# Remainder rows of k and v: four heads on each half of the partitions, multiplied in quarters of the array

## The chip, the cores and the metric

The kernel runs on one core of a Trainium2 chip. The metric is the device time of one execution in microseconds (us), as a median over runs; lower is better. The core has TensorE (PE in the profile, with PEld for its weight loads), VectorE (DVE), ScalarE (ACT), GpSimd (POOL) and SyncE (SP), whose queue issues most of the DMA transfers.

## What is computed

A linear attention block without softmax, a root-mean-square norm, and then an MLP mixer over tokens and channels. All inputs are f32 or wider, all results f32.

```python
batch, n_heads, seq, head_dim = (8, 8, 576, 64)      # q, k, v
d_tok, d_ch = (256, 1536)                            # the mixer's weights
kv = np.einsum('bhsd,bhse->bhde', k, v)
out = np.einsum('bhsd,bhde->bhse', q, kv)
rms = np.sqrt(np.mean(out * out, axis=-1, keepdims=True) + 1e-06)
x = (out / rms * g_norm)                             # then (B,H,S,D) -> (B,S,H*D)
h = np.maximum(x.transpose(0, 2, 1) @ w_tok1, 0.0) @ w_tok2
u = x + h.transpose(0, 2, 1)
y = u + np.maximum(u @ w_ch1, 0.0) @ w_ch2
```

The step of interest is `kv`: for each batch and head, k transposed times v, a sum over 576 rows that gives 64 by 64.

## The kernel before

Batches are worked in four pairs; the two of a pair are its sides 0 and 1. A batch's k is held as `k_in[side]`, 128 partitions by 5 row groups by 512 columns (8 heads of 64), and v as `v_in[side]`. `J` = 4 of the groups hold rows 0 to 511, four rows to a partition; the fifth (`JJ` = 5) holds the remainder, the last `HF` = 64 rows. The two buffers of a side are used again by every pair, so the batches of pair n+1 are loaded (`load`, steps `l0`, `l1`) after the products of pair n have read them. `load` issues four things on SP's queue in this order: k's 512 rows (1 MB), k's remainder, v's 512 rows, v's remainder. In the first pair (b < 2) the remainder takes another way: 64 rows of k and v are laid on 128 partitions as half rows and spread out with zeros by `spread_k`. From pair 1 on `load_rem` puts the 64 remainder rows on partitions 0 to 63, all 512 columns, in two transfers of 32 rows by 2 KB. Partitions 64 to 127 of that group are zero: `zero_rows` clears them once on POOL during pair 0 (steps `zz0`, `zz1`).

`kv(side, half)` multiplies for four heads (`half` 0: columns 0 to 255, `half` 1: columns 256 to 511). Each matmul takes 128 rows and 64 columns of k as weights and 64 columns of v as moving operand, and goes to one column half of the array (`h` 0 or 1, output partitions 0 to 63 or 64 to 127), so that two run side by side. Per half there are 2 x 5 x 2 = 20 matmuls, per batch 40, 8 of them for the remainder group, over 128 partitions of which 64 are zero. The two halves accumulate in two PSUM tiles of the pool `kv`. `evict` (steps `e00` to `e11`) copies each to `kvp[side]` on ScalarE, and `attend` multiplies q by it, as 64 x 64 matmuls that go round the four quarters of the array.

The order of all work is written out by hand in lists of step names: `start` (pair 0), `middle` (pair 1 beside the token mixing of pair 0), `steady` (pairs 2 and 3). The steps that are named below: `kvSH` k by v of side S, half H; `eSH` its copy; `aC` the attention of row chunk C (`a4` the remainder rows of q); `qCH`, `gCH`, `tCH` squares on ScalarE, gain and sum on VectorE; `dCT` and `sCT` the scaling of chunk C on VectorE or ScalarE, `pCT` on POOL; `hST` the first product of the token mixing, `hr` its remainder rows and ReLUs, `uN` the second product of tile N with its addition and store; `-` before a name is a step of the pair before; `fN` fetches a block of the channel weights, a number plays that many steps of their decoding on ScalarE and VectorE. Every matmul is issued by one helper, line 136 of the profile; SP's DMAs by line 124, ScalarE's plain copies by line 133. Each engine does its instructions in the order in which they are issued.

Of the kernel before, what the change touches and what calls it, by code (L numbers as in the profile page):

```python
# [20 lines left out]
def kernel(  # L21
# [32 lines left out]
    nc = tc.nc  # L54
    P = 128
    B, S, DM = k.shape
    D = g_norm.shape[0]
# [3 lines left out]
    J, JJ, HF, Q = 4, 5, 64, 32  # L61
    LO = P * J
# [3 lines left out]
    DH = DM // 2  # L66
# [41 lines left out]
    k_in = [inp.tile([P, JJ, DM], F32, name=f"k_in{i}") for i in range(2)]  # L108
    v_in = [inp.tile([P, JJ, DM], F32, name=f"v_in{i}") for i in range(2)]
# [5 lines left out]
    def do(f, *a, **kw):  # L115
        return lambda: f(*a, **kw)
# [4 lines left out]
    keep = tc.keep_in_program_order  # L121

    def dma(o, i, engine=nc.sync):
        keep(engine.dma_start(o, i))
# [10 lines left out]
    def matmul(*a, **kw):  # L135
        keep(nc.tensor.matmul(*a, **kw))  # L136
# [7 lines left out]
    def load_rem(dst, t, b):  # L144
        if b < 2:
            at = ds(DH if dst is k_in[b] else 0, DH)
            dma(v_in[b][:, J, at], t[b, LO:].rearrange("r (a d) -> (r a) d", a=2))
            return
        for n in range(0, HF, Q):
            dma(dst[n:n + Q, J], t[b, LO + n:LO + n + Q].rearrange("(r e) d -> e r d", e=8))  # L150

    def load(b):

        if b >= B:
            return

        pairs = ((k_in[b % 2], k), (v_in[b % 2], v))
        if b > 1:
            for dst, t in pairs:
                load_rows(dst, t, b)  # L160
                load_rem(dst, t, b)
        else:
            for f in (load_rows, load_rem):
                for dst, t in pairs:
                    f(dst, t, b)
# [119 lines left out]
    def t_sums(b):  # L285

        def step(o, x, y):
            return lambda: tensor_add(b(o), b(x), b(y), ALU.subtract)

        return [step(5, 7, 1), step(6, 3, 5), step(7, 3, 7), step(4, 2, 6)]  # L290
# [96 lines left out]
    def attention(pair, groups):  # L387


        bank, stat, kv_ps = {}, {}, {}  # L390
# [4 lines left out]
        whole = pair == 0  # L395

        def kv(side, half, js=range(JJ)):
            kk, vv = k_in[side], v_in[side]
            if js[0]:
                o = kv_ps[side, half]  # L400
            elif whole:
                o = kv_ps[side, half] = zeroed[half]
            else:
                o = kv_ps[side, half] = ps["kv"].tile([P, 2, P], F32, name="ps_kv", tag="kv")
            split = len(js) < JJ
            for i in range(2):
                for j in js:
                    for h in range(2):
                        at = ds(half * DH + i * P + h * D, D)
                        matmul(o[ds(h * D, D), i, ds(h * D if whole else 0, D)], lhsT=kk[:, j, at],  # L410
                               rhs=vv[:, j, ds(i * P + h * D, D) if whole and j == J else at],
                               start=(j == 0 and not (split and i)), stop=(j == JJ - 1), skip_group_check=True)

        def evict(side, half):
            n = P if whole else D
# [156 lines left out]
        steps = {}  # L572
        for s in range(2):
            for h in range(2):
                steps |= {f"ka{s}{h}": do(kv, s, h, range(J)), f"kb{s}{h}": do(kv, s, h, range(J, JJ)),
                          f"kv{s}{h}": do(kv, s, h), f"e{s}{h}": do(evict, s, h),
                          f"l{s}": do(load, 2 * pair + 2 + s)}
            steps |= {f"lq{s}": do(load_q, 2 * pair + 2 + s), f"lr{s}": do(load_q_rest, 2 * pair + 2 + s)}
        for c in range(5):
            if whole:  # L580
# [740 lines left out]
    def play(lines, after={}, **stages):  # L1321

        for name in " ".join(lines).split():
            if name.isdigit():
                for _ in range(int(name)):
                    next(stages["rounding"], lambda: None)()
            elif name[0] == "-":
                stages["before"][name[1:]]()  # L1330
            else:
                next(stages[s][name] for s in ("attention", "mixing", "more")
                     if name in stages.get(s, ()))()
# [32 lines left out]
        else:  # L1366
            keep(nc.scalar.activation(o, i, AF.Copy, scale=own[:, half:half + 1]))

    def zero_rows(side):
        for t in (k_in, v_in):  # L1370
            keep(nc.gpsimd.memset(t[side][HF:, J], 0.0))

    root = stats.tile([P, 1], F32, name="root")
    keep(nc.vector.memset(root, 1.0))
    keep(nc.scalar.activation(root, root, AF.Sqrt))
    def spread_g():
# [3 lines left out]
        copy(g_sb[:, 0], o[:, :D])  # L1380

    start = [
# [6 lines left out]
    middle = [  # L1389
# [5 lines left out]
    steady = [[  # L1395
# [10 lines left out]

    attentions = [attention(0, ((0,), (1,), (2,), (3,), (4,)))]
    attentions += [attention(p, ((0, 1), (2, 4), (3,))) for p in range(1, B // 2)]

    mixings = [token_mixing(p, (2, 4, 6)) for p in range(B // 2 - 1)]  # L1410
    mixings.append(token_mixing(B // 2 - 1, range(2, 9), (0, 1)))
    more = {f"w{n}{k}": f for n, b in enumerate(first_rows[:1] + tok1[1:] + tok2 + first_rows[1:]) for k, f in enumerate(b)}
# [6 lines left out]
    def keep_warm(n):  # L1419
# [3 lines left out]
        for _ in range(n):  # L1423
# [2 lines left out]
    more |= {f"j{n}": do(keep_warm, n) for n in (4, 5, 21)}  # L1426
    more["gs"] = spread_g
    more |= {f"zk{side}{half}": do(spread_k, side, half) for side in range(2) for half in range(2)}
    more |= {f"zz{side}": do(zero_rows, side) for side in range(2)}
    play(start, attention=attentions[0], mixing=mixings[0], more=more)  # L1430
    play(middle, attention=attentions[1], mixing=mixings[0], before=attentions[0],
         more=more, rounding=rounding)
    for n in range(1, B // 2 - 1):
        play(steady[n - 1], attention=attentions[n + 1], mixing=mixings[n], before=attentions[n] | {"u8": mixings[n - 1]["u8"]},
             more=more, rounding=rounding)
# [16 lines left out]
    more = {f"c{i}": f for i, f in enumerate(t_sums(lambda n: uT[0][:, SB[n]]))}  # L1452
# [98 lines left out]
```

## Time and profile before

| | us |
|---|---|
| median of 3 runs (769.81 to 770.58) | 770.58 |
| the profiled execution | 769.76 |
| its span | 767.9 |
| k by v, 640 records in all, ScalarE's 15 copies of it | 20.9 and 266 ns each |

The profile is one execution on the chip, with the start and length of every instruction. The granted TensorE clock is full throughout. The span falls in two parts: up to about 151 us the attention and the first three pairs' mixing over tokens, thereafter the last pair's mixing and the mixing over channels. The change touches the first part alone, from pair 1 (its first k by v starts at 36 us) to pair 3 (its last at 130 us).

How to read it: the page gives each engine's busy time; the chain of waits goes back from the last instruction to what released it; views in order of time list start, length, engine, line, what is written and read, and a count, and in square brackets the idle time before with its releaser. Engine names with a q are the queue, where DMAs are issued. A form such as 128*64 is the part of the array that a matmul uses, rows by columns.

### The profile page before, as it was taken

To read this page: it belongs to the slowest core of one execution; us is meant where nothing else is said; L and a number is where in the kernel's file an instruction comes from. 1 tells how busy PE (TensorE), PEld (TensorE's weight loads), DVE (VectorE), ACT (ScalarE), POOL (GpSimd) and SP (SyncE) were. 2 spreads that over 40 slices of the span, in tenths; PEclk is the share of its full clock that TensorE was granted. 3 is DMA by queue.
4 is the path that set the end of the run, shared out by engine and by line. 5 is a ranking of instruction groups with operands and counts; after the bars stand their busy time and mean duration, and the time that the engine had idled before them with its cause. 6 is when DMAs were issued, how large, how long until landed. Compare 5 with 4: busy or idle time off the path is not lost.

```text
span 767.9 us, 12737 instructions
## 1 busy us (share of the span) xinstructions
PE 761.9 (99%) x4694; PEld 615.4 (80%) x4694; DVE 644.9 (84%) x958; ACT 279.5 (36%) x563; POOL 112.8 (15%) x125
## 2 busy tenths in 40 slices
PE   9999999999999999999999999999999999999997
PEld 8655555446888888888888888888888888888887
DVE  4868886997757779899968989997898997798996
ACT  3656666773210332512234241123352223325221
POOL 1003030204410000002240002042000227000204
PEclk9999999999999999999999999999999999999999
DMA  9999997599699785589997578999659889755679
GB/s 356 379 366 382 353 376 281 178 326 340 244 290 318 291 284 167 172 271 217 221 230 251 154 226 213 261 185 265 195 154 295 159 227 211 199 150 158 156 188 120
DMA packets 137981, 188.28 MB, mean 245 GB/s; under 512 B 48704, under 2 KB 95808, under 8 KB 135872
## 3 DMA queue, kind: packets, MB, share of 16 engines
q1 hardware_dynamic: 102240, 168.72, 68.3%
q0 software_dynamic: 34848, 18.36, 15.9%
q8 instruction: 38, 0.62, 0.3%
q10 hardware_dynamic: 832, 0.39, 0.2%
q14 instruction: 23, 0.19, 0.1%
HBM read 138.28 MB, written 49.15 MB: 244 GB/s over the span
## 4 chain that ended last, share of the span: by engine, by line
PE 96%; DMA 2%; DVE 1%; SPq 0%; ACT 0%; issue 0%; DVEq 0%
PE ps_d L136 28%; PE ps_b L136 19%; PE ps_a L136 19%; PE ps_u L136 8%; PE ps_h L136 8%; PE ps_v L136 5%; PE ps_c L136 3%; PE ps_w L136 2%; PE ps_kv L136 2%; PE ps_o L136 2%; DMA raw<-in_moe_w_tok_dram 1%; DMA v_in<-in_k_dram 1%; PE ps_r L136 0%; DVE x L494 0%; DVE ms L522 0%; DVE w_tok L211 0%
## 5 line engine op out<-in xcount | busy, mean ns | idle before, releaser
L136 PE MATMUL ps_d<-ui,w 128*128 128x256 f32 x504 | 118.6, 379 | 0.0
L136 PEld LDWEIGHTS ps_d<-ui,w 128*128 128x128 f32 x504 | 96.0, 190 | 12.8
L133 ACT COPY ps_d<-ps_a 128x768 f32<-128x768 f32 (+1 forms) x56 | 32.0, 572 | 199.9 <-PE ps_a L136 196.9
L127 DVE TENSOR_TENSOR v<-v,v 128x1536 f32<-128x1536 f32 (+2 forms) x70 | 103.3, 1483 | 0.3
L136 PE MATMUL ps_b<-sv,w 128*128 128x256 f32 x324 | 78.9, 380 | 0.0
L136 PE MATMUL ps_a<-v,w 128*128 128x256 f32 x324 | 78.8, 379 | 0.0
L1275 POOL DMA_DIRECT2D out_dram<-us x24 | 26.8, 1835 | 291.8 <-ACT p L133 286.5
L136 PEld LDWEIGHTS ps_b<-sv,w 128*128 128x128 f32 x324 | 61.3, 190 | 8.8 <-issue 0.6
L136 PEld LDWEIGHTS ps_a<-v,w 128*128 128x128 f32 x324 | 61.7, 190 | 8.2
L136 PE MATMUL ps_u<-h,w_tok 128*128 128x512 f32 (+1 forms) x160 | 64.7, 599 | 0.0
L136 PE MATMUL ps_d<-v,w 128*128 128x256 f32 x258 | 62.7, 379 | 0.0
L130 ACT ACTIVATE v<-v 128x768 f32<-128x768 f32 (+1 forms) x54 | 42.6, 822 | 55.1 <-DVE v L127 52.3
L136 PE MATMUL ps_h<-x,w_tok 128*128 128x512 f32 x128 | 57.6, 601 | 0.7 <-DVE w_tok L211 0.6
L1275 POOL DMA_DIRECT2D out_dram<-r x40 | 41.3, 1926 | 102.0 <-ACT p L133 80.3
L136 PE MATMUL ps_d<-sv,w 128*128 128x256 f32 x228 | 55.4, 379 | 0.0
L136 PEld LDWEIGHTS ps_d<-v,w 128*128 128x128 f32 x258 | 49.1, 190 | 6.5
L136 PEld LDWEIGHTS ps_u<-h,w_tok 128*128 128x128 f32 (+1 forms) x160 | 25.7, 179 | 31.1 <-issue 26.7
L136 PEld LDWEIGHTS ps_d<-sv,w 128*128 128x128 f32 x228 | 43.4, 190 | 5.8
L136 PE MATMUL ps_a<-uT,w 128*128 128x256 f32 x192 | 46.7, 379 | 0.0
L136 PEld LDWEIGHTS ps_h<-x,w_tok 128*128 128x128 f32 x128 | 23.5, 190 | 28.3 <-issue 24.3
L136 PE MATMUL ps_b<-ui,w 128*128 128x256 f32 x168 | 40.9, 379 | 0.0
L136 PEld LDWEIGHTS ps_a<-uT,w 128*128 128x128 f32 x192 | 36.5, 190 | 4.9
(178 smaller groups left out, 1299.1 us busy)
## 6 DMA issues: line engine op xcount, KB each, us to landing
w<-parts SPq DMA_DIRECT2D x168, 384.0 KB
w<-parts SPq DMA_DIRECT2D x56, 192.0 KB
uT<-blocks SPq DMA_DIRECT2D x36, 256.0 KB
k_in<-in_k_dram SPq DMA_DIRECT2D x8, 1024.0 KB
v_in<-in_v_dram SPq DMA_DIRECT2D x8, 1024.0 KB
qT<-in_q_dram SPq DMA_DIRECT2D x8, 1024.0 KB
out_dram<-x POOLq DMA_DIRECT2D x16, 512.0 KB, 7.2
raw<-in_moe_w_ch_dram SPq DMA_DIRECT2D x8, 768.0 KB
```

The lines of the kernel that those rows point to most:

```text
L127: keep(engine.tensor_tensor(out=o, in0=a, in1=b, op=op))
L130: keep(nc.scalar.activation(o, a, AF.Relu))
L133: keep(nc.scalar.copy(o, a))
L136: keep(nc.tensor.matmul(*a, **kw))
L1275: keep(nc.gpsimd.dma_start(to, t()[ds(b * Q, Q), at].rearrange("p n l j -> p n (l j)"), accum_op=ALU.add))
```

## The change

The remainder rows of pairs 1 to 3 are laid out another way: heads 0 to 3 on partitions 0 to 63, heads 4 to 7 on partitions 64 to 127, 256 columns each. So a batch's remainder of k comes in four transfers of 32 rows by 1 KB, and so does v's; nothing is cleared. `kv` leaves out the remainder group in these pairs, and a new step `kr0` or `kr1` (`kv_rem`) multiplies it for both halves: 8 matmuls of 64 rows by 64 columns, in which the halves of the heads stand on the row halves of the array and the two heads of a pair on the column halves. It adds to both accumulators, so both copies `e` follow it. In the lists `kr` stands behind both `kv` steps of its side; at side 0 of pairs 2 and 3 the step `-u8` is moved between `kv01` and `kr0`, ahead of the copies and `-d40`, and `-a3` then follows `kr0` on TensorE.

```diff
@@ load_rem
-        for n in range(0, HF, Q):
-            dma(dst[n:n + Q, J], t[b, LO + n:LO + n + Q].rearrange("(r e) d -> e r d", e=8))
+        for a in range(2):
+            for n in range(0, HF, Q):
+                dma(dst[ds(a * HF + n, Q), J, :DH],
+                    t[b, ds(LO + n, Q), ts(a, DH)].rearrange("(r e) d -> e r d", e=8))
@@ kv
-                               start=(j == 0 and not (split and i)), stop=(j == JJ - 1), skip_group_check=True)
+                               start=(j == 0 and not (i and (split or not whole))),
+                               stop=(j == JJ - 1), skip_group_check=True)
+
+        def kv_rem(side):
+            o = [kv_ps[side, a] for a in range(2)]
+            for i in range(2):
+                for h in range(2):
+                    for a in range(2):
+                        r, at = ds(a * HF, HF), ds(i * P + h * D, D)
+                        matmul(o[a][ds(h * D, D), i, :D], lhsT=k_in[side][r, J, at], rhs=v_in[side][r, J, at],
+                               start=False, stop=True, skip_group_check=True)
@@ the steps
-                          f"kv{s}{h}": do(kv, s, h), f"e{s}{h}": do(evict, s, h),
+                          f"kv{s}{h}": do(kv, s, h, range(JJ if whole else J)), f"e{s}{h}": do(evict, s, h),
...
+            steps[f"kr{s}"] = do(kv_rem, s)
@@ the first pair (zz1 likewise)
-    def zero_rows(side):
-        for t in (k_in, v_in):
-            keep(nc.gpsimd.memset(t[side][HF:, J], 0.0))
...
-        "j21 zk00 zk01 ka00 ka01 gs kb00 e00 kb01 e01 zz0 eg0 eg1 l0 w01 w02 w03 w04 j4",
+        "j21 zk00 zk01 ka00 ka01 gs kb00 e00 kb01 e01 eg0 eg1 l0 w01 w02 w03 w04 j4",
@@ middle
-        "h100 h110 h101 h111 w31 w22 w23 w24", "kv00 e00 -lq1 w32 w33 w34",
-        "h102 h112 h103 h113 w41 w42 w43 w44", "kv01 e01", "hr l0 z2",
+        "h100 h110 h101 h111 w31 w22 w23 w24", "kv00 -lq1 w32 w33 w34",
+        "h102 h112 h103 h113 w41 w42 w43 w44", "kv01 kr0 e00 e01", "hr l0 z2",
...
-        "kv10 kv11 e10 e11 t10 t11 m0 r0 lq0", "u3 z6 i0 d00 s01 d11 f1", "u4 l1", "a2 q20 g21 q21 g20",
+        "kv10 kv11 kr1 e10 e11 t10 t11 m0 r0 lq0", "u3 z6 i0 d00 s01 d11 f1", "u4 l1", "a2 q20 g21 q21 g20",
@@ steady, both lists alike
-        "kv00 kv01 e00 e01 -d40 f3", "-u8 -a3 -q30 -g31 -q31 -g30 -t30 -t31 -m3 -r3 -lq1",
+        "kv00 kv01 -u8 kr0 e00 e01 -d40 f3", "-a3 -q30 -g31 -q31 -g30 -t30 -t31 -m3 -r3 -lq1",
...
-        "h11 1 x11 1", "hr z2 f5 f6", "a1 q10 g11 q11 g10 lq0", "kv10 kv11 e10 e11 t10 t11 m0 r0", "u0 i0 1",
+        "h11 1 x11 1", "hr z2 f5 f6", "a1 q10 g11 q11 g10 lq0", "kv10 kv11 kr1 e10 e11 t10 t11 m0 r0", "u0 i0 1",
```

More of the change, by code (lines that the diff above doesn't have):

```diff
@@ L1428 @@
     more |= {f"zk{side}{half}": do(spread_k, side, half) for side in range(2) for half in range(2)}
-    more |= {f"zz{side}": do(zero_rows, side) for side in range(2)}
     play(start, attention=attentions[0], mixing=mixings[0], more=more)
```

6 rows, old and new, of tables (start, steady) are left out of this document.

## The prediction

> **What bounds the kernel now.** I read the page's busy line and its chain first, then the list of what TensorE waited for over the whole run.
>
> ```profile
> span 767.9 us, 12737 instructions
> PE 761.9 (99%) x4694; PEld 615.4 (80%) x4694; DVE 644.9 (84%) x958; ACT 279.5 (36%) x563; POOL 112.8 (15%) x125
> ...
> PE 96%; DMA 2%; DVE 1%; SPq 0%; ACT 0%; issue 0%; DVEq 0%
> ```
>
> ```profile
> PE ps_j L136 <- DVE ones L1353: 1.1, 1, 1.1
> PE ps_h L136 <- DVE w_tok L211: 0.6, 1, 0.6
> ```
>
> ```profile
> 27.65 1.99 PE L136 MATMUL ps_h<-x,w_tok 128*128 128x512 f32 x4 [0.62 <-DVE w_tok L211]
> ```
>
> TensorE is busy 99% of the span, carries 96% of the chain, and of its only two waits the later ends at 27.65 us, before the edit's first matmul. From there to the end one matmul follows the other. So an edit is worth what it adds to or takes from TensorE's own string of matmuls, plus any wait that it brings in where there is none now. The edit's place in that string is the next thing to read: the chain in order of time (start, length, piece).
>
> ```profile
> 36.00 1.32 PE ps_kv L136 x40
> 37.32 3.63 PE ps_h L136 x8
> 40.95 1.31 PE ps_kv L136 x40
> 42.27 1.92 PE ps_h L136 x8
> 44.18 1.09 PE ps_o L136 x64
> ...
> 51.71 2.48 PE ps_kv L136 x80
> 54.20 3.63 PE ps_u L136 x8
> 57.83 1.09 PE ps_o L136 x64
> 58.92 0.47 PE ps_r L136 x32
> 59.38 5.35 PE ps_u L136 x12
> 64.73 2.48 PE ps_kv L136 x80
> 67.21 1.72 PE ps_u L136 x8
> 68.93 1.09 PE ps_o L136 x64
> ...
> 78.18 8.98 PE ps_h L136 x24
> ```
>
> An f32 matmul leaves two records, so x80 is the 40 matmuls of one batch and x40 is half a batch.
>
> **Rates and the price of a switch.** Two lengths of k by v give its rate: (2.48 - 1.315) / 40 = 0.029 us a record, and 1.315 - 40 x 0.029 = 0.15 us that a group pays once, whatever its length. The quarter-array groups give theirs: ps_r follows ps_o in the same form, 0.47 / 32 = 0.0147 us a record with nothing paid once; ps_o then is 64 x 0.0147 = 0.94, and 0.15 once. ps_u of 8 and of 12 records: 0.43 each and 0.19 once. But `u8` (ps_u x8 at 67.21), which has k by v's form (two halves by columns), takes 1.72 = 4 pairs x 0.43, nothing once. So the 0.15 to 0.2 belongs to a change of the array's form, not to a new group.
>
> **Part 1, the matmuls.** Per batch, 8 of 40 matmuls (16 records) leave the halves: -16 x 0.029 = -0.466 us. They come back as 16 quarter records: 16 x 0.0147 = 0.235, and 0.15 for the added switch: +0.385. What follows pays its own switch as before, except at side 0 of the last two pairs. There `u8` stays behind k by v in one form, `kr0` comes next, and `a3` (quarters) follows `kr0` in its own form, so that ps_o's 0.15 is dropped.
> - Both sides of pair 1, side 1 of pairs 2 and 3: 4 x (-0.466 + 0.385) = -0.32 us.
> - Side 0 of pairs 2 and 3: 2 x (-0.466 + 0.385 - 0.15) = -0.46 us.
>
> Together -0.78 us. The bounds: no switch is paid for the new group at all, 6 x (-0.466 + 0.235) - 2 x 0.15 = -1.69; the quarters are no faster than the halves, 4 x 0.15 = +0.6 (side 0 of the last two pairs breaks even). I take the middle, because `kr`'s matmuls have `attend`'s form, 64 x 64 with row halves alternating and two accumulators, whose rate was just read.
>
> By itself stands a rule of the Trainium skill, "TensorE: Matmul & The Clock Gate", in the section "Wait — 56ns, not 53.3ns?": starts of matmuls never come closer than about 25 ns. By that a `kr` group would be estimated at 16 x 25 ns and the switch, 0.55, and the part at +0.2 us instead of -0.78. This trace does not agree for quarters: 32 records in 0.47.
>
> **Part 2, waits at `kr`.** In the built program `kr`'s first two matmuls wait for four loads each; before, one matmul within k by v waited for four. Such waits show as semaphore instructions in TensorE's load queue (between 51.6 and 54.3 us, a count, then min/median/max ns):
>
> ```profile
> L136 PEldq EVENT_SEMAPHORE  x3: 51/51/51, 51.7 to 53.7; - x3
> ```
>
> Three of them lie in a group that still took 2.48, as the one at 64.73 did: the queue runs ahead. All of TensorE's string stands behind them. From below 0, from above six for each batch all exposed, 6 x 6 x 0.051 = +1.8 us. I take +0.1, near the row.
>
> **Part 3, later copies.** Both copies of a batch's k by v now start after `kr`. In pair 1, side 0, they used to stand apart; the tight one is `a0`, which needs both, and behind it on ScalarE the ReLUs of `hr`.
>
> ```profile
> 42.31 0.27 ACT L133 COPY kvp<-ps_kv 128x128 f32<-128x128 f32 x1 [0.64 <-PE ps_kv L136]
> 43.36 0.60 ACT L130 ACTIVATE h<-ps_h 128x512 f32<-128x512 f32 x1 [0.78 <-PE ps_h L136]
> ```
>
> `kr0` ends about 42.2; two copies of 0.27 are done by 42.8; `hr` (ps_h at 42.27) covers them until 44.1. Lead 1.3 us, cost 0; without `hr` it would be 0.27, one copy. At side 1 (k by v at 51.71) the copies end near 54.7 and `a2` starts at 57.83. At side 0 of pair 2 (64.73), `kr0` ends at 64.73 + 2.01 + 1.72 + 0.385 = 68.85, and ScalarE made these copies only at 68.91 anyway:
>
> ```profile
> 68.91 0.41 ACT L133 COPY kvp<-ps_kv 128x128 f32<-128x128 f32 x2
> ...
> 76.44 2.02 ACT L557 ACTIVATE x<-x,inv 128x64 f32<-128x64 f32 x8 [1.03 <-DVE inv L541]
> ```
>
> **Part 4, `u8` moved.** Its matmuls, VectorE's addition and three stores on POOL's queue now stand ahead of `kr0`, the copies and `d40`. On VectorE only the addition and `d40` change places:
>
> ```profile
> 71.29 0.69 DVE L566 TENSOR_TENSOR x<-x,inv 128x512 f32<-128x512 f32 x1
> 71.89 0.68 DVE L127 TENSOR_TENSOR x<-ps_u,x 128x512 f32<-128x512 f32 x1
> 72.49 1.28 DVE L494 TENSOR_TENSOR x<-ps_o,g_sb 128x512 f32<-128x512 f32 x2
> ```
>
> `u8`'s matmuls are over at 68.93, so at 71.29 neither waits and L494 behind them starts as before. What hangs on L494 is late next: `s30` (ScalarE, 76.44 to 78.46) feeds the third matmul of `h10`, four records and a switch after 78.18, near 80.1. TensorE is about 0.4 us earlier there; 1.6 us of lead are enough. Cost 0. No store passes another on POOL, and the order on it is otherwise kept.
>
> **Part 5, POOL's clearing goes.**
>
> ```profile
> L1371 POOL MEMSET k_in<- x2: 519/520/520, 11.6 to 21.5; 64x512 f32 x2
> ```
>
> Two such and two of v_in, with TensorE and SP's first reload (20.75) waiting for none: 0.
>
> **Part 6, the loads.** Each remainder comes in four transfers of 32 rows by 1 KB instead of two by 2 KB, so 24 more issues on SP (count, then min/median/max ns of one):
>
> ```profile
> L124 SPq DMA_DIRECT2D k_in<-in_k_dram x20: 328/695/1089, 0.8 to 93.9; - x20
> ```
>
> Four more for a batch cost 4 x 0.695 = 2.8 us of SP's time and push all that is queued behind them: qT, the raw weights, the blocks. The tightest batch is the first reloaded one:
>
> ```profile
> 20.75 2.42 SPq L124 DMA_DIRECT2D k_in<-in_k_dram x3
> 24.09 2.49 SPq L124 DMA_DIRECT2D v_in<-in_v_dram x3
> 26.68 0.85 SPq L124 DMA_DIRECT2D raw<-in_moe_w_tok_dram  x2
> ...
> 32.28 2.22 SPq L124 DMA_DIRECT2D v_in<-in_v_dram  x3
> ...
> 44.37 1.90 SPq L124 DMA_DIRECT2D v_in<-in_v_dram  x3
> ```
>
> ```profile
> 0.00:30.00 30.00, 28.21 (x304) 23.99 (x306) 17.67 (x47) 12.95 (x33) 3.36 (x11) 1.00 0.98 357
> ```
>
> Up to its v the transfers in SP's order add up to 10.7 MB, and 30 us at 357 GB/s (last column) move 10.7 MB: landed about 30, needed at 36.00. Two extra issues stand ahead of v's rows, 2 x 0.7 = 1.4 us, at most 2 x 1.09 = 2.2. Lead 6 us: cost 0. The next two batches are all issued by 34.5 and 46.3 and used at 51.71 and 64.73, 17 us and more ahead. The w_tok2 words behind batch 2 (1.2 MB, so landed near 33) come up to 3 us later, and ScalarE reads them only here:
>
> ```profile
> 38.90 0.71 ACT L181 ACTIVATE w_tok<-raw 128x576 f32<-128x576 f32 x1
> ```
>
> **The sum.** -0.78 + 0.1 = -0.7 us. The profiled execution took 769.76 (span 767.9 and 1.9 around it); the median of the runs shown is 770.58, 0.8 above it. On the median: 770.58 - 0.7 = 769.9 us.
>
> **Rivals.**
> A, the switches are free: the array need not empty for `kr`, -1.69 us, 768.9. For it: `u8` and ps_r pay nothing. Against: both keep the form of what precedes them, and every group of the chain that changes it pays. 0.15; with some gain I do not see, 0.20 for faster by over 0.2% (1.54 us, about what a measurement of this kernel can tell from no change).
>
> B, the new group is no faster, or its waits show: +0.6 (quarters one pair at a time), or -0.78 + 1.8 = +1.0 with all semaphore instructions exposed: 771.2 to 771.6. For it: `kr` has only 8 matmuls to hide its waits in. Against: ps_r's 0.47 and the row of part 2. 0.15, and it stays within 0.2%.
>
> C, loads late, on the slower side. In the program each issue on SP waits for the transfer eight issues earlier, and more small transfers leave fewer bytes under way.
>
> ```profile
> SPq L124 <- DMA k_in<-in_k_dram: 14.1, 7, 4.1
> ```
>
> Were each of the two transfers added ahead of batch 2's v rows held for the longest such wait, 4.1 us, v would come 8.2 us later, 2.2 beyond its lead, and TensorE would stand at 36.00: -0.7 + 2.2 = +1.5 there, and as much again if batch 3 runs dry: 772 to 774. It decides from 6 us of lateness on. Against: an issue takes 0.7 and these waits already lie inside the issue times above. 0.14.
>
> The rule that speaks for C stands in "DMA: Bandwidth & Descriptors" of the Trainium skill, section "Bandwidth": transfers under 64 KB are dominated by their descriptors, and these go from 64 to 32 KB. From its table (0.95 us at 64 KB, 0.68 at 4 KB) I would estimate some 3 us more of transfer time for a load, half the lead; no run here shows it yet.
>
> **Numbers.** The forecast itself, about -0.7 us, 0.51; B 0.15; both within 0.2%: 0.66. Faster 0.20, slower 0.14. The likeliest case's own range is 769.3 to 770.5. A's and B's ends, 768.9 and 771.6, are the bounds of the unknown costs; the runs shown differ by 0.8 among themselves, half of which goes on A's side: 768.5 to 771.6.
>
> **What would show it.** In the chain of the changed kernel: k by v of 64 records at 2.0 us and of 32 at 1.08; a group of 16 at 0.39, or 0.24 under A, 0.6 under B; ps_o behind `kr0` at 0.94 instead of 1.09; `u8` still 1.72. The list of TensorE's waits should still hold two rows; a third, for k_in or v_in, would be C. A shift of more than 1 us from 260 us on, where nothing is edited, would prove the forecast wrong.

## The result, and the profile after

| | us |
|---|---|
| before, median of 10 runs (769.70 to 770.58) | 770.17 |
| after, median of 10 runs (768.13 to 768.99) | 768.46 |
| ratio, with its 95% interval | 0.9979 (0.9969 to 0.9989) |
| the profiled execution of after, and its span | 768.43, 766.6 |

The change makes the kernel faster by 1.7 us, 0.21% with an interval of 0.11 to 0.31%. Part of the distance to the 769.9 of the forecast lies in its base: it was put on 770.58, the median of three runs, where ten give 770.17. The step itself was forecast as -0.7 us and came out at -1.7; 1.0 us is to be found.

The page of after, its line of the span and its busy line:

```profile
span 766.6 us, 12767 instructions
PE 761.2 (99%) x4694; PEld 613.0 (80%) x4694; DVE 644.5 (84%) x958; ACT 279.0 (36%) x563; POOL 110.8 (14%) x121
```

TensorE is 0.7 us less busy, and still busy throughout. Its string, from the chain of after in order of time (start, length, piece):

```profile
36.33 1.08 PE ps_kv L136 x32
...
41.05 1.47 PE ps_kv L136 x48
...
51.97 2.41 PE ps_kv L136 x80
...
59.10 0.63 PE ps_r L136 x32
...
65.08 2.02 PE ps_kv L136 x64
67.09 1.72 PE ps_u L136 x8
68.81 0.39 PE ps_kv L136 x16
69.20 0.93 PE ps_o L136 x64
...
88.36 2.41 PE ps_kv L136 x80
...
129.74 2.41 PE ps_kv L136 x80
```

The reader sets each group beside its row of before. Side 0 of pair 1: 1.08 + 1.47 where 1.32 + 1.31 stood, -0.08. The three sides 1: 2.41 for 2.48, -0.07 each. Side 0 of pairs 2 and 3: 2.02 + 0.39 + 0.93 for 2.48 + 1.09, -0.23 each, with `u8` between at its old 1.72 (pair 3 has the same four lengths from 106.45 on). Together -0.75 us. One group is longer, ps_r of pair 1 with 0.63 for 0.47. In the second execution of the same program (below) it took 0.47 again, but in `keep_zero`, `split_loads` and `kr_first` 0.56, 0.56 and 0.76; all of these bring the remainder of a tensor in four transfers, and in no profile with two was it longer. Its cause is open.

What TensorE waited for in after:

```profile
PE ps_j L136 <- DVE ones L1366: 1.1, 1, 1.1
PE ps_h L136 <- DVE w_tok L213: 0.6, 1, 0.6
PE ps_kv L136 <- DMA v_in<-in_v_dram: 0.4, 1, 0.4
```

The third row is not the one that rival C named: it lies at 8 us, at the first load of the program, which the change does not touch. No wait was added from pair 1 on.

So the string gives 0.75 us, and it arrives at the end. From the first k by v of pair 1 to the start of the last pair's mixing before takes 115.07 us (36.00 to 151.07) and after 114.47 (36.33 to 150.80), of which 0.16 is ps_r. Between the two profiled executions that start moves by 0.27 only, because after had begun its k by v 0.33 later, and the last matmuls and additions move by the same 0.26. (In the profiles of these two kernels and of `keep_zero`, `split_loads` and `two_loads` this start lies anywhere from 36.00 to 36.74, and no run here ties it to the change.) These rows are VectorE's last addition, of before and of after:

```profile
763.70 0.29 DVE L127 TENSOR_TENSOR xs<-ps_d,xs 128x128 f32<-128x128 f32 x1 [0.38 <-PE ps_d L136]
```

```profile
763.44 0.29 DVE L127 TENSOR_TENSOR xs<-ps_d,xs 128x128 f32<-128x128 f32 x1 [0.38 <-PE ps_d L136]
```

But the spans differ by 1.3 us. From the end of that addition to the end of the span before takes 767.94 - 763.99 = 3.95 us and after 766.62 - 763.73 = 2.89. There nothing is computed: the last stores land, SP waits for them, and the engines meet at a last barrier. Part of this is chance (when the last store lands); one thing is not. The transfers of each kernel between 766 and 769 us, behind its last store, are these (the busy tenths of the engines in 40 slices of 75 ns; queue: packets, MB, share); first before, then after:

```profile
DMA  0000000000000000000020000000000004000000
## 3 DMA queue, kind: packets, MB, share of 16 engines
q14 instruction: 2, 0.02, 1.8%
```

```profile
DMA packets 0, 0.00 MB, mean 0 GB/s; under 512 B 0, under 2 KB 0, under 8 KB 0
```

Before fetches two blocks of instructions of 8 KB each at the very end, at 767.5 and at 768.5, the second behind the span's own end of 767.94; after fetches none there. In the single records of SP and POOL a pause goes with each: of 0.36 and 0.12 us in SP's last waits, of 0.3 us in POOL's last barrier. (After has one of 0.36 us in SP's waits too, but right at the last landing.) From the landing of the last store to the end, before takes 2.15 us and after 1.37.

The theory to be tested was therefore: 0.75 us come from the matmuls, as the prediction's part 1 had it, and about as much from the end of the program, because the change lengthens SP's stream of instructions (24 issues) and shortens POOL's (four clearings), so that neither comes to a new block of instructions behind the last store. Rivals: that the second half also lies among the matmuls, or in chance.

### The profile page after: what moved, and what is told of

Its sections match the earlier page's. It is cut to its first block, busy times and chain, and to the rows that moved or that the text cites. A ratio compares the mean times of both kernels' runs of the same rounds, so it can differ in the third digit from the quotient of the medians.

```text
span 766.6 us, 12767 instructions
## 1 busy us (share of the span) xinstructions
PE 761.2 (99%) x4694; PEld 613.0 (80%) x4694; DVE 644.5 (84%) x958; ACT 279.0 (36%) x563; POOL 110.8 (14%) x121
## 4 chain that ended last, share of the span: by engine, by line
PE 96%; DMA 2%; DVE 1%; SPq 0%; ACT 0%; issue 0%; DVEq 0%
PE ps_d L136 28%; PE ps_b L136 19%; PE ps_a L136 19%; PE ps_u L136 8%; PE ps_h L136 8%; PE ps_v L136 5%; PE ps_c L136 3%; PE ps_w L136 2%; PE ps_kv L136 2%; PE ps_o L136 2%; DMA raw<-in_moe_w_tok_dram 2%; DMA v_in<-in_v_dram 1%; PE ps_r L136 0%; DVE x L506 0%; DVE ms L534 0%; DVE w_tok L213 0%
```

## The experiments

All times are medians in five rounds beside the kernel before on the same chip, with the ratio and its interval. Each kernel's edit is against after unless it says otherwise.

**The two kernels again.** `aa_before` and `aa_after` are the kernels before and after, unchanged.

> The kernel before, unchanged, against itself. All theories: ratio 1.000 within 0.1%. It tells how large the last stretch is by chance, from VectorE's last addition to the end of the span: 3.9 us in the profile of before, 2.9 in that of after. If that stretch belongs to the program, it is 3.9 again; if it is chance, it may come out anywhere from 2.9 to 3.9.

> The changed kernel, unchanged. Theory 1 (the gain on TensorE's string is the forecast 0.75 us, the rest of the measured 1.7 lies at the end of the program): the string of k by v, u8 and a3 as in the first profile (2.02 + 1.72 + 0.39 + 0.93 at side 0 of pair 2), the last stretch 2.9 us again, and a ratio of 0.9975 to 0.9985. Theory 2 (the last stretch is chance): the same string, a last stretch above 3.3, and a ratio near 0.999, -0.8 us. Also whether ps_r of pair 1 takes 0.63 again or 0.47.

`aa_before`: 770.12, ratio 0.9998 (0.9990 to 1.0007). `aa_after`: 768.81, ratio 0.9982 (0.9973 to 0.9991), -1.34 us. The groups of `aa_after` are those of after, with ps_r at 0.47; from its first k by v to the last pair's mixing it takes 114.30 us, `aa_before` 115.06. What the method can't see is some 0.7 us. The whole last stretch, from VectorE's last addition to the end of the span, was 3.76 us in `aa_before` and 3.44 in `aa_after`, where 3.9 and 2.9 had been expected. Its first part, to the landing of the last store, scatters, as the second theory had it: 1.80 and 1.63 us in the two of before, 1.52 and 2.05 in the two of after. The part behind the last landing comes again: two fetches of instructions from 766 us on in `aa_before` and 2.13 us, none in `aa_after` and 1.39 (the table below).

**Is it the quarters of the array?** `one_row_half` keeps the split in halves and quarters, but its remainder lies on partitions 0 to 63 with all 512 columns, as before, and comes in two transfers as before, so that `kr` uses one row half of the array only (the edit of the loads is left out here).

```diff
-                        r, at = ds(a * HF, HF), ds(i * P + h * D, D)
+                        r, at = ds(0, HF), ds(a * DH + i * P + h * D, D)
```

> The changed kernel with the remainder rows where they were before (partitions 0 to 63, all 512 columns, two transfers of 2 KB rows): kr then uses the upper row half of the array alone, two matmuls side by side instead of four. If the gain is the four quarters: a kr group of 16 records takes 0.15 + 16 x 0.029 = 0.62 us instead of 0.39, six times, +1.4 us against the changed kernel, and slower than before by 0.6. If a kr group's length comes from its weight loads or its issue and not from the rows it lies on: 0.39 stays, and the time is that of the changed kernel or a little less, since 24 transfers fewer are issued.

770.83, ratio 1.0011 (1.0002 to 1.0020): slower than before. In its chain:

```profile
41.02 1.74 PE ps_kv L136 x48
...
52.20 2.67 PE ps_kv L136 x80
```

0.26 to 0.27 more than after for the 16 records of one `kr`, and six times that is 1.6 us: the whole gain of the string and more. (The rest of the 2.0 to 2.4 us above after and `aa_after` lies at the end, where one fetch is back; see the table below.) So a pair of column halves of 64 rows is no faster than one of 128 rows; what pays is that the two row halves run side by side. This was the prediction's rival B as a kernel of its own.

**Is it `u8` moved?** `no_u8` puts `u8` back behind the copies.

```diff
-        "kv00 kv01 -u8 kr0 e00 e01 -d40 f3", "-a3 -q30 -g31 -q31 -g30 -t30 -t31 -m3 -r3 -lq1",
+        "kv00 kv01 kr0 e00 e01 -d40 f3", "-u8 -a3 -q30 -g31 -q31 -g30 -t30 -t31 -m3 -r3 -lq1",
```

> The changed kernel with u8 put back behind kr0, the copies and d40, as its place was. If each change of the array's form is paid (0.15 us for quarters, about 0.2 for the halves with 512 columns): at side 0 of pairs 2 and 3 k by v 2.02, kr0 0.39, u8 1.9 instead of 1.72, a3 1.09 instead of 0.93, so +0.35 each, +0.7 us against the changed kernel (ratio to before 0.9985 to 0.999). If switches are free (rival A): 1.72 and 0.93 stay, no difference to the changed kernel.

769.18, ratio 0.9989 (0.9980 to 0.9997). Its rows of side 0 of pair 2, from the view of TensorE in order of time, have two more changes of form, from k by v's halves to `kr0` and back to `u8`:

```profile
64.82 2.48 PE L136 MATMUL ps_kv<-v_in,k_in 128*64 128x64 f32 x80
67.22 1.94 PE L136 MATMUL ps_u<-h,w_tok 128*64 128x512 f32 x8
69.09 1.16 PE L136 MATMUL ps_o<-kvp,qT 64*64 64x64 f32 x64
```

From the start of k by v to 70.18, where the next group starts, it takes 5.36 us; in after the same work goes from 65.08 to 70.13, 5.05. So the order spares 0.3 us a time, both switches that the prediction's rate gives (0.15 each). And a wait showed up that after had only just escaped:

```profile
PE ps_o L136 <- DMA qT<-in_q_dram: 0.5, 1, 0.5
```

It is the last qT, in pair 3, late by the longer SP queue (below). The two together are 0.6 + 0.5, more than the 0.4 to 0.7 by which its median stands above after and `aa_after`. The profiled execution, 770.26, was the longest of its eleven, 1.1 above their median; such a wait need not come in every run.

**Is it the end of the program?** Three kernels. `keep_zero` is after with the clearing on POOL, which nothing needs there: POOL's stream is as before, SP's as after.

```diff
+    def zero_rows(side):
+        for t in (k_in, v_in):
+            keep(nc.gpsimd.memset(t[side][HF:, J], 0.0))
...
```

> The changed kernel with the four clearings on POOL kept (they clear rows that the loads then fill). After the last addition of before and of its repeat, two instruction fetches show (queue q14), POOL waits 0.3 us in the last barrier and SP 0.4; of the changed kernel none. Theory 1 (the end of the program depends on where each engine's instructions end in its 8 KB fetches): with POOL's four instructions back, one fetch and POOL's 0.3 us come back, +0.3 us against the changed kernel, and nothing else moves. Theory 2 (the clearings cost at the start, by holding the first reload back): +0.3 or more before 36 us, no fetch at the end. If neither: the changed kernel's time.

769.24, ratio 0.9991 (0.9982 to 1.0000). TensorE's string is that of after, and one fetch is back:

```profile
q14 instruction: 1, 0.01, 0.8%
```

So four instructions on POOL in the first 25 us decide whether a block is fetched at 767.9, 1.0 us behind the span's end of 766.90. Within the span no pause shows, 1.38 us from the last landing to the end. The price lies outside it: the time of an execution is longer than its span, by 1.77 to 1.86 us in all 21 executions of after and `aa_after`, and by 2.17 to 2.27 in all eleven of `keep_zero`. That is 0.4 us, the lower of the 0.4 to 0.8 by which its median stands above the two of after. What is done in the time outside the span no profile here shows.

`split_loads` is the kernel before with the loads of after, without the quarters: four transfers of 32 rows by 1 KB into partitions 0 to 63, the clearing kept.

```diff
+        for a in range(2):
+            for n in range(0, HF, Q):
+                dma(dst[n:n + Q, J, ts(a, DH)],
+                    t[b, ds(LO + n, Q), ts(a, DH)].rearrange("(r e) d -> e r d", e=8))
```

> The kernel before with each remainder loaded in four transfers of 32 rows by 1 KB, on the partitions where it was; its matmuls as before. TensorE's groups: 2.48, 1.32 and 1.09 as before. Theory 1 (end of the program): SP's stream is longer by 24 issues, one of the two last fetches goes, and SP's 0.4 us with it: -0.4 us against before, less what the loads cost. Rival C (loads late): qT of the last batch is issued near 129 us instead of 120, TensorE waits for it at a2 of pair 3 (it is needed there near 137.8), 0 to 1 us. So 0.9990 to 1.0005 of before.

769.87, ratio 0.9999 (0.9991 to 1.0008). The groups are those of before but for ps_r at 0.56, TensorE waits for no load from pair 1 on, and one fetch is left, by the length of the streams POOL's. The profile has the end of `keep_zero`: 1.38 us from the last landing, the fetch 1.0 us behind the span's end, and 2.17 to 2.26 us outside the span in all eleven executions, where the kernel before has 1.79 to 1.97. By these figures its end is some 0.4 us shorter than before's; the interval, 0.7 us below before to 0.6 above, holds that and can't show it.

`before_end` is the kernel before with streams of SP and POOL as long as those of after: four transfers of 16 rows by 2 KB a tensor, and the clearing on VectorE.

```diff
-        for n in range(0, HF, Q):
-            dma(dst[n:n + Q, J], t[b, LO + n:LO + n + Q].rearrange("(r e) d -> e r d", e=8))
+        for n in range(0, HF, Q // 2):
+            dma(dst[n:n + Q // 2, J], t[b, LO + n:LO + n + Q // 2].rearrange("(r e) d -> e r d", e=8))
...
-            keep(nc.gpsimd.memset(t[side][HF:, J], 0.0))
+            keep(nc.vector.memset(t[side][HF:, J], 0.0))
```

> The kernel before with two things of the change that touch no matmul: the remainder of k and v comes in four transfers of 16 rows by 2 KB a tensor (as many issues on SP, and as many bytes in each, as after), and VectorE clears the unused half in place of POOL (four instructions of some 0.3 to 0.6 us in the first pair). So the instruction streams of SP and POOL are as long as those after, while TensorE's string is that of the kernel before. Theory that half of the gain lies in the end of the program (no instruction fetch after the last addition): groups of k by v at 1.32, 1.32, 2.48, 2.48, 2.48, 2.48 as before, last addition at about 764.0 to 764.3, no fetch behind it, about 769.4, 0.75 below the kernel before. Rival, that all of the gain lies among the matmuls: 770.2, no change. Were the clearing on VectorE to hold TensorE up in the first pair, k by v would start later than 36.0 us, by as much.

770.90, ratio 1.0012 (1.0003 to 1.0020), +0.9 us: the 769.4 was missed, because the condition in its last sentence came true. VectorE's clearing stands ahead of the decoding of w_tok, on which TensorE waits in pair 0. Its waits, and its last addition:

```profile
PE ps_h L136 <- DVE w_tok L211: 1.8, 1, 1.8
```

```profile
765.34 0.29 DVE L127 TENSOR_TENSOR xs<-ps_d,xs 128x128 f32<-128x128 f32 x1 [0.38 <-PE ps_d L136]
```

TensorE waits 1.2 us longer than before, k by v starts at 37.64 for 36.00, and this lateness goes unchanged to the last addition: 765.34 for 763.70, or for 763.96 in `aa_before`, 1.4 to 1.6 us. The time is only 0.9 longer. No instruction is fetched behind the last addition, the last landing lies 1.37 us before the end, 1.77 to 1.92 us lie outside the span, and the end is shorter by 0.5 to 0.8 us, with not one matmul changed. That is the second half of the gain, in a kernel that has nothing of the first.

The ends together (us), of the profiled executions; outside the span is the execution's time less its span, and the sum is that of the two columns before it:

| | last addition ends | span ends | fetches behind it | last landing to the end | outside the span | sum |
|---|---|---|---|---|---|---|
| before, `aa_before` | 763.99, 764.25 | 767.94, 768.01 | 2, 2 | 2.15, 2.13 | 1.82, 1.92 | 3.97, 4.05 |
| after, `aa_after` | 763.73, 763.96 | 766.62, 767.40 | 0, 0 | 1.37, 1.39 | 1.81, 1.82 | 3.18, 3.21 |
| `before_end` | 765.63 | 768.65 | 0 | 1.37 | 1.83 | 3.20 |
| `keep_zero`, `split_loads` (POOL's) | 763.66, 764.22 | 766.90, 767.36 | 1, 1 | 1.38, 1.38 | 2.21, 2.21 | 3.59, 3.59 |
| `two_loads` (below), `one_row_half` (SP's) | 763.43, 765.14 | 767.12, 768.72 | 1, 1 | 1.73, 1.86 | 2.11, 2.11 | 3.84, 3.97 |

With no fetch the sum is 3.2 us in three kernels, with both 4.0, with POOL's alone 3.6 and with SP's alone 3.8 to 4.0. So the two fetches together go with 0.8 us, and their shares don't simply add. Nor does a fetch behind the span always lengthen the time outside it: before's second one lies there too, but POOL's pause is within the span, and the time outside is near that of after. Whose a fetch is has been taken from the lengths of the streams; the record of the fetch doesn't name the engine.

**Fewer or more transfers.** `two_loads` brings the remainder of a tensor in two transfers of 64 rows by 1 KB, `eight_loads` in eight of 16 rows, `one_load` in one of 128 partitions (the lines that these replace are left out).

```diff
two_loads
+            dma(dst[ds(a * HF, HF), J, :DH], t[b, LO:, ts(a, DH)].rearrange("(r e) d -> e r d", e=8))
eight_loads
+            for n in range(0, HF, Q // 2):
+                dma(dst[ds(a * HF + n, Q // 2), J, :DH],
+                    t[b, ds(LO + n, Q // 2), ts(a, DH)].rearrange("(r e) d -> e r d", e=8))
one_load
+        dma(dst[:, J, :DH], t[b, LO:].rearrange("r (a d) -> a r d", a=2))
```

> The changed kernel with one transfer of 64 rows by 1 KB for each half of the heads, two for a tensor as before, instead of four. TensorE's groups as in the changed kernel. SP: qT of the last batch issued near 120 us again instead of 129, no wait of TensorE on a load from 30 us on. End of the program: SP's stream has before's length, so one fetch and SP's 0.4 us come back (as in the kernel with one row half): 0 to +0.4 us against the changed kernel. If instead the late loads cost TensorE time in the changed kernel, this one is faster by it.

769.14, ratio 0.9985 (0.9976 to 0.9994). The string is that of after; the last qT is issued at 124.25 us where after has 129.25; one fetch is back at the end, SP's, with 2.07 to 2.24 us outside the span in all eleven executions. The median is not told apart from that of after.

> The change with eight transfers of 16 rows by 1 KB a tensor in place of four of 32: 48 more issues on SP than after. Theory of the queue (each issue waits for the transfer eight issues earlier, and smaller ones leave fewer bytes under way): the qT of the last pair, issued at 129.25 us after, comes 4 to 9 us later and is needed at about 137.5 with 3 us of transfer, so TensorE stands for 0.5 to 5 us at the first ps_o of that chunk, and perhaps at the k by v of the last pair; 769 to 774. The forecast's own sum (lead enough, an issue costs SP time alone): no third row in the list of TensorE's waits from the edit on, 768.5 to 768.9 as after.

797.83, ratio 1.0351 (1.0336 to 1.0365): 27.8 us slower, far beyond the 774 that was expected at most. The DMA rows from 20 to 60 us, one digit (busy tenths of the 16 engines) and one rate for each us, of after and of `eight_loads`:

```profile
DMA  9999999989626999999999984397999989989799
GB/s 389 367 285 260 298 348 344 320 336 418 246 81 102 355 419 390 397 401 442 434 389 353 336 339 176 108 270 181 386 399 436 420 294 255 352 324 434 307 302 335
```

```profile
DMA  9999998410097941066999999961026999715198
GB/s 383 375 284 272 293 346 328 156 49 16 16 172 319 459 167 30 25 79 230 396 419 378 393 440 399 418 233 50 4 66 197 385 401 365 272 47 119 34 184 305
```

The engines run dry: at 29, 36 and 48 us they move 4 to 25 GB/s. The chain of `eight_loads` says why:

```profile
39.28 8.86 DMA k_in<-in_k_dram
48.14 0.02 issue
48.16 0.68 SPq L124
...
54.48 1.99 DMA v_in<-in_v_dram
...
56.61 0.51 PE ps_kv L136 x14
```

SP's issues take eight semaphores in turn, so an issue waits for the transfer eight issues earlier. With eight small transfers behind k's rows, the last of the eight waits until those rows have landed (8.86 us). Only behind it are v's rows, the next megabyte, issued, at 48.88, where k's were issued at 39.28: with the small ones of k landed, little was left under way. Then the eight small ones of v go out at 0.7 us each; the last is issued at 54.48 and lands 1.99 us later, and TensorE's k by v goes on at 56.61. In after four small ones lie between two big ones, so that the next big one goes out while the last is still landing (of the same batch, k's rows at 32.62 and v's at 36.23); the dips at 31 and 45 us (81 and 108 GB/s) are the same thing in small. This is rival C, at twice the count.

> The change with the whole remainder of a tensor in one transfer (128 partitions by 1 KB, 128 KB): 12 issues fewer on SP than before, 36 fewer than after, and kr waits for one load of k and one of v in place of four each. TensorE: groups of 2.0, 0.39 and ps_o 0.93 as after if the waits are hidden there, as the theory has it; the last qT issued some 8 us earlier than after, near 120 us. The end of the program: SP's stream is shorter, so where its fetch falls is open; 768.5 with none, 769.2 with one behind the last addition.

789.74, ratio 1.0256 (1.0242 to 1.0270): missed by 20 us. Fewer issues did not bring the loads forward. From 20 to 60 us again:

```profile
DMA  9999999999998999999411197971615698999979
GB/s 383 372 292 267 307 330 373 374 322 334 311 370 303 396 313 340 360 382 416 178 54 51 51 176 297 427 216 49 161 62 138 211 347 181 384 376 432 426 332 205
```

Several slices stand at one tenth of the engines and 50 GB/s. Here the outermost extent of the source is 2, in all other versions 8, and the plateau is what two of sixteen engines would give; that the outermost extent deals the rows out to the engines is read from this plateau and was not varied further. The loads then come late to TensorE by way of the decoding on ScalarE:

```profile
PE ps_u L136 <- ACT h L130: 7.1, 1, 7.1
```

**Can the waits at `kr` show?** `kr_first` puts the quarters of side 1 ahead of the halves, straight behind `a1`, whose form they share, so that one change of form falls away. `kr_first_one` is the same with the one transfer of `one_load`, so that `kr`'s first matmuls wait for one load each.

```diff
...
-        "a1 q10 g11 q11 g10", "kv10 kv11 kr1 e10 e11 t10 t11 m0 r0", "u0 f11 i0 1", "u1 z4 d00 s01", "u2",
+        "a1 q10 g11 q11 g10", "kr1 kv10 kv11 e10 e11 t10 t11 m0 r0", "u0 f11 i0 1", "u1 z4 d00 s01", "u2",
...
```

> The changed kernel with kr1 ahead of kv10 and kv11 in pairs 1 to 3, right behind a1, whose form (quarters) it shares; it then starts the accumulation. If a change of form costs 0.15 us and an unchanged form nothing: ps_kv x80 at side 1 takes 16 x 0.0147 + 0.15 + 64 x 0.029 = 2.25 us instead of 2.41, three times, -0.48 us against the changed kernel (ratio to before 0.9970 to 0.9978). If kr's cost is fixed by its own waits or loads (rival B): 2.41 stays.

768.89, ratio 0.9985 (0.9976 to 0.9993), no better than after, and its groups of 80 records are longer, not shorter: 2.49 in the chain for 2.41, where 2.25 had been expected. In the single records the second matmul of `kr` comes 0.14 us late, behind two semaphore instructions of 51 ns.

> As kr_first (at side 1 the quarters go ahead of the halves, straight behind a2, so that one change of form falls away), with one transfer a tensor, so that kr's first two matmuls wait for one load each. Theory that kr_first's 2.49 us for 80 records was made of exposed waits behind a quarter group: with a third or half of the semaphore instructions the 80 records take 2.25 to 2.40. Rival, that the change from kr to the halves costs more than elsewhere whatever it waits for: 2.49 again. The time: 768.2 to 768.9 without a fetch behind the last addition, up to 0.7 more with one.

790.35, ratio 1.0258 (1.0244 to 1.0272), for the reason of `one_load`. But its group at side 1 of pair 2 waited for no load and can be read. TensorE in order of time, of after, `kr_first` and `kr_first_one`:

```profile
87.20 1.16 PE L136 MATMUL ps_o<-kvp,qT 64*64 64x64 f32 x64
88.29 2.48 PE L136 MATMUL ps_kv<-v_in,k_in 128*64 128x64 f32 x80
90.70 1.55 PE L136 MATMUL ps_u<-h,w_tok 128*128 128x512 f32 x3
```

```profile
87.24 1.16 PE L136 MATMUL ps_o<-kvp,qT 64*64 64x64 f32 x64
88.22 2.67 PE L136 MATMUL ps_kv<-v_in,k_in 64*64 64x64 f32 x80
90.82 1.55 PE L136 MATMUL ps_u<-h,w_tok 128*128 128x512 f32 x3
```

```profile
98.61 1.16 PE L136 MATMUL ps_o<-kvp,qT 64*64 64x64 f32 x64
99.59 2.43 PE L136 MATMUL ps_kv<-v_in,k_in 64*64 64x64 f32 x80
101.95 2.41 PE L136 MATMUL ps_u<-h,w_tok 128*128 128x512 f32 x5
```

From the start of ps_o to the start of ps_u: 3.50, 3.58 and 3.34 us. With two loads to wait for in place of eight, the same order takes 0.24 us less and beats after by 0.16, about the switch that it spares. The group of pair 3 bears this out in small only: from the start of ps_o at 139.87 to the end of its 80 records at 143.46 it takes 3.59 us, where the same stretch is 3.41 in pair 2, 3.65 in `kr_first` and 3.57 in after. So the waits of part 2 can show where `kr` follows a quarter group (by 0.24 us in one group, 0.06 in the other), and are hidden where it follows the halves. An order like this with two transfers a tensor, as in `two_loads`, would be the next candidate, worth at most three times 0.16 us. It was not tried.

## Why the prediction was right, and where it was short

The mechanism that was forecast held, but it makes only about half of the gain. That the whole, 768.46, lies at the lower end of the range (768.5) is luck: that end was put there for rival A, free switches, which did not come true, and the case's own range, 769.3 to 770.5, was missed; 0.4 us of that is the base. The prediction had also named a sign of being wrong, a shift of more than 1 us from 260 us on. In the first pair of profiles the last addition shifts by 0.26 and the end of the span by 1.32 (in the second pair by 0.29 and 0.61), so by its own sign it was wrong about the end.

- **Part 1, the matmuls: right.** -0.78 forecast, -0.75 in the chain; k by v of 64 records at 2.02 (2.0 forecast), of 32 at 1.08, the group of 16 at 0.39, ps_o behind `kr0` at 0.93 (0.94), `u8` at 1.72. The price of a switch is borne out twice: `no_u8` pays two more in each of two places, 0.3 us. Rival A would have shown 0.24 for the group of 16; rival B is what `one_row_half` does.
- **Part 2, the waits: right, by luck of the place.** +0.1 was taken; nothing shows in the groups of after. That TensorE's load queue runs ahead was read from two groups of 2.48 us, which was no comparison: the one at 64.73 holds two of these semaphore instructions as well. It holds there all the same, by `two_loads`, where `kr` waits for half as many loads and the groups are still 1.47, 2.41 and 0.39; in `kr_first` it didn't behind a quarter group, where `kr`'s second matmul came 0.14 us late.
- **Parts 3 and 4: right.** No wait for a copy of k by v, no wait for VectorE or ScalarE from pair 1 on.
- **Part 5, the clearing at 0: right for what it looked at, short as a whole.** It asked who waits for the four instructions in pair 0, and nobody does. It did not ask what fewer instructions on POOL move at the other end of the program.
- **Part 6, the loads: the cost 0 held, its term was too small.** The prediction added 0.7 us for each issue, 2.8 us for a batch. But an issue that waits eight issues back adds up along the program. SP's rows of pair 3 in after:

```profile
105.42 11.34 SPq L124 DMA_DIRECT2D v_in<-in_v_dram  x5
116.81 1.01 SPq L124 DMA_DIRECT2D qR<-in_q_dram  x2
...
129.25 0.38 SPq L124 DMA_DIRECT2D qT<-in_q_dram  x1
```

  That qR was issued at 97.40 before, and that qT at 120.44: 19 and 9 us late. The qT is needed at 137.5, and the 8.2 us from issue to need just held; in `no_u8`, where the transfer landed 8.83 us behind its issue, they did not. The prediction looked for the tightest batch at the first reload and found lead there, and did not follow the lateness to the last pair.
- **The sum: it left out a term.** It ran from the first edited matmul to the last, and took all that lies behind for fixed. The end of the program gave 0.5 to 0.8 us (`before_end`; 2.15 for 1.37 in the profiles), and -0.75 - 0.75 = -1.5 stands between the -1.34 and -1.71 that were measured. With POOL's four instructions back the end is 0.4 us longer (`keep_zero`), without SP's 24 added issues 0.6 to 0.8 (one profile each of `two_loads` and `one_row_half`), and with both as before 0.8. Not shown is that the engine waits for the fetch itself: the pauses come 0.6 to 0.9 us ahead of the recorded transfers, and the fetches of `keep_zero` and `split_loads` come when the span is over.

## What to carry to other kernels

On a kernel whose TensorE never waits, price an edit by the records and by each change of the array's form, and put groups of one form side by side; 0.6 of the 0.75 us of this change's string hung on the place of one group (`no_u8`). Before cutting a transfer into smaller ones, count the issues between two big ones against the number that may be under way, since the step from four to eight small ones cost 28 us where that from two to four cost nothing that the medians show. An edit that changes only the number of instructions on an idle engine can still move the end by 0.4 us (`keep_zero`), so an effect of that size needs the profile's last microseconds, and the time less the span, read beside its middle.

## What had not been expected of the hardware

- Instruction fetches at the end: two blocks of 8 KB behind the last store in both executions of before, none in after, with 2.15 and 1.37 us from the last landing to the end. In `keep_zero` and `split_loads`, whose profiles have the only fetch 1.0 us behind the span's end, the time outside the span is 0.4 us longer in all eleven executions of each.
- Matmuls of 64 rows on one row half are no faster than those of 128 rows: 16 records took 0.65 us in `one_row_half` (2.67 - 2.02), and 16 x 0.029 + 0.15 = 0.61 at the rate of 128 rows; with both row halves in use they take 0.39.
- Semaphore instructions on TensorE's load queue (51 ns each) were hidden behind matmuls of 128 rows by 64 columns (2.41 us for the group of 80 in after and in `two_loads`, which has half the loads to wait for) and exposed behind those of 64 by 64: three quarters of the waits of one `kr` cost 0.24 us in one group and 0.06 in another (`kr_first` against `kr_first_one`).
- A transfer with an outermost extent of 2 held the engines at one tenth and 50 GB/s for whole slices, as none with 8 did in after.
